# v of twelve attention pairs as two scaled 16-bit floats instead of three bfloat16 parts

## Chip, cores and metric

The kernel runs on one core of one Trainium2 chip. The metric is the device time of one execution in microseconds (us); three runs of the kernel before stand in the table below. A program is recorded ahead of time with a scheduling layer, which fixes the order of the instructions on every engine; on the chip each engine takes its own instructions strictly in that order and waits on semaphores for the others.

## The reference

Three blocks follow each other. Inputs are float32, the output is float32.

- Attention over 4 batches x 12 heads, 448 positions, head dimension 64, causal: `softmax(mask(q k^T / 8)) v`, with 1e-9 added to the sum of each row.
- A token and channel mixer on the result x (4 x 448 x 768): `u = x + (relu(x^T w_tok1) w_tok2)^T`, then `u + relu(u w_ch1) w_ch2`, with 1536 channels inside.
- A second mixer: `theta = x w_theta`, `y = w_tok_r (x cos theta) + w_tok_i (x sin theta)`, `u = x + y`, output `u + relu(u w_ch)`.

The change concerns the last product of the attention, attention weights times v, in half of its heads.

## The kernel before

Two heads of a batch make a pair, so there are 24 pairs, numbered 0 to 23 in order of batch. A pair has seven tiles of queries (`TILES`): one that holds the first 64 queries of both heads, and for each head three of 128 queries. The main loop goes through 24 x 7 = 168 steps. In each step the scores of one tile are computed (PE, L331 and L333), masked and reduced on DVE (L338), and put through the exponential on ACT (L340). Four steps later (`LAG`) the product with v of that tile is made (`pv`). After the seventh tile of a pair `finish` divides by the row sums, and after every second pair the token mixer (`tokmix`, L411 to L430) uses the result.

Between the steps stand the *units* of the channel mixer, each of 18 matmuls of 448 columns (L227 to L229), which fill PE. The same loop converts the weights (`round_first`, `round_bits`, `round_split`): they come in 64 bit, are rounded to float32 on ACT and DVE, scaled by a power of two found on the chip (`power`) and split into two float16 parts.

PE works in float32 only at a lower rate. So the pairs 0 to 11 multiply v as float32 (L375), and the pairs 12 to 23 work in pieces of 16 bit. There the weights of a tile are scaled by 2^15 and written as two float16 parts, "hi" by ACT (L157) and the rest by DVE (L360), into the tile `ph`; a transposing DMA on the SP queue brings them to `pt` (L363). v is cut into three bfloat16 parts (L296 to L301): the upper half of each float32 word is the first part and is read in place, DVE subtracts it into `v_mid` and the upper half of that is the second part, and DVE subtracts again for the third, in the lower half of `v_mid`. Per block of keys the product is then made of five matmuls of 64 columns (L386): hi with all three parts, the rest with the first two.

`v_raw` has two buffers and `v_mid` one; the parts of a pair are cut in `prep`, which is recorded in the first step of the pair before. `pv` and `scores` are recorded with high priority. `power` sums squares with matmuls of one column against ones, takes half the exponent on DVE (L140), inverts it (L127) and makes the factors on POOL (`product`, L130).

Of the kernel before, what the change touches and what calls it, by code (L numbers as in the profile page):

```python
# [18 lines left out]
P = 128  # L19
# [35 lines left out]
def fused(ctx, tc, q, k, v, w_tok1, w_tok2, w_ch1, w_ch2, w_theta, w_tok, w_ch, out):  # L55
# [73 lines left out]
    def product(dst, a, b, c):  # L129
        nc.gpsimd.tensor_scalar(out=dst, in0=a, scalar1=b, scalar2=c, op0=ALU.mult, op1=ALU.mult)  # L130

    def power(p, s, sq):

        ps = mm_bank()
        n = sq.shape[-1]
        nc.tensor.matmul(ps[:, 0:1], lhsT=ones, rhs=tiny, start=True, stop=False)
        for j in range(n):
            nc.tensor.matmul(ps[:, 0:1], lhsT=ones, rhs=sq[:, j:j + 1], start=False, stop=j == n - 1)
        g = main.tile([P, 2], F32, tag="g", name="g", bufs=4)
        nc.vector.tensor_scalar(out=g[:, 0:1].bitcast(U32), in0=ps[:, 0:1].bitcast(U32), scalar1=1, scalar2=EXPONENT,  # L140
                                op0=ALU.logical_shift_right, op1=ALU.bitwise_and)
        two_over(g[:, 1:2], g[:, 0:1])
        product(s, g[:, 1:2], 2.0 ** -51, 1.0)
        product(p, g[:, 0:1], 2.0 ** 64, 1.0)

    def largest(p, ps):
        nc.vector.tensor_reduce(out=p, in_=ps, axis=mybir.AxisListType.X, op=ALU.max)
# [119 lines left out]
    def prep(b, pr):  # L267
        qr = ap2.tile([P, 2 * S], F32, tag="qk_raw", name="q_raw", bufs=2)
        if b * NPR + pr in NATIVE:
            kr = ap2.tile([P, 2 * S], F32, tag="kh", name="k_pad")  # L270
            for t, src in ((kr, k), (qr, q)):
                (nc.vector if b * NPR + pr == 0 else nc.gpsimd).memset(t[64:128], 0.0)
                if b * NPR + pr == 0 and t is qr:
                    for c in (slice(0, 2 * P), slice(2 * P, 2 * S)):
                        nc.scalar.dma_start(out=t[0:64, c], in_=src[b, pr, 0:64, c])
                else:
                    loads[b * NPR + pr] = nc.sync.dma_start(out=t[0:64], in_=src[b, pr, 0:64])
        else:
            loads[b * NPR + pr] = nc.sync.dma_start(out=qr, in_=q[b, pr])
            kr = ap2.tile([P, 2 * S], F32, tag="qk_raw", name="k_raw", bufs=2)  # L280
            nc.sync.dma_start(out=kr, in_=k[b, pr])
        vr = ap2.tile([P, 9 * D], F32, tag="v_raw", name="v_raw")
        nc.sync.dma_start(out=vr, in_=v[b, pr])
        if b * NPR + pr in NATIVE:
            qs, kh, kl = qr, kr, None
        else:
            qs = ap2.tile([P, 2 * S], F32R, tag="qs", name="qs")
            copy_to(pick("qhi"), qs, qr)
            rest_to(pick("qlo"), qs[64:128], qr[64:128], qs[64:128])
            kh = ap2.tile([P, 2 * S], F32R, tag="kh", name="kh")  # L290
            copy_to(pick("khi"), kh, kr)
            kl = ap2.tile([P, 2 * S], F32R, tag="kl", name="kl")
            rest_to(pick("klo"), kl, kr, kh)
        if b * NPR + pr in NATPV:
            return qs, kh, kl, (vr,)
        v1 = vr.bitcast(BF16).rearrange("p (n w) -> p n w", w=2)[:, :, 1]  # L296
        vm = ap2.tile([P, 9 * D], F32, tag="v_mid", name="v_mid", bufs=1)
        rest_to(pick("v"), vm, vr, v1)
        v2, v3 = (vm.bitcast(BF16).rearrange("p (n w) -> p n w", w=2)[:, :, z] for z in (1, 0))
        rest_to(pick("v"), v3, vm, v2)  # L300
        return qs, kh, kl, (v1, v2, v3)  # L301

    TILES = ((0, 0), (1, 0), (1, 1), (2, 0), (2, 1), (3, 0), (3, 1))

    class Pair:
        def __init__(self, b, pr, parts):
            self.b, self.pr = b, pr
            self.qs, self.kh, self.kl, self.v = parts
            self.mx = ap2.tile([P, 7], F32, tag="mx", name="mx")
            self.sm = ap2.tile([P, 8], F32, tag="sm", name="sm")  # L310
            self.pts, self.ps, self.sent = {}, None, None
            self.native_pv = b * NPR + pr in NATPV
# [53 lines left out]
    def pv(pp, i, h):  # L366
# [9 lines left out]
                                 start=(u == 0), stop=(u == len(blks) - 1))  # L376
            return
        if i == 0:
            jobs = [(0, c, 8) for c in range(3)] + [(1, c, 8) for c in range(2)]
        else:  # L380
            jobs = [(0, c, 6 + h) for c in range(3)]
            for u in range(i):
                jobs += [(1 + u, c, 2 * u + h) for c in range(3)]
                jobs += [(1 + i + u, c, 2 * u + h) for c in range(2)]
        for n, (blk, c, vt) in enumerate(jobs):
            pp.pv = nc.tensor.matmul(pp.ps[:, reg:reg + D], lhsT=pt[:, blk], rhs=pp.v[c][:, vt * D:(vt + 1) * D],  # L386
                             start=(n == 0), stop=(n == len(jobs) - 1))

    def finish(pp, xb, xg):
        ps, sm = pp.ps, pp.sm  # L390
        nc.vector.tensor_scalar(out=sm[:, 0:7], in0=sm[:, 0:7], scalar1=1e-9, scalar2=1.0 if pp.native_pv else PSC, op0=ALU.add, op1=ALU.mult)
        nc.vector.reciprocal(out=sm[:, 0:7], in_=sm[:, 0:7])
        nc.vector.tensor_tensor(out=xb[:, 1:4, :].rearrange("p i (h d) -> p (i h) d", h=2),
                                in0=ps[:, D:7 * D].rearrange("p (j d) -> p j d", d=D),
# [205 lines left out]
    for n, (b, pr, t) in enumerate(steps):  # L600
# [24 lines left out]
        if t == 0 and (b, pr) != (B - 1, NPR - 1):  # L625
            nx = (b + (pr + 1) // NPR, (pr + 1) % NPR)
            with tc.high_priority(AHEAD), ExitStack() as es:
                if nx == (0, 1):
                    es.enter_context(tc.issue_after(loads[0].ins))
                parts[nx] = prep(*nx)  # L630
        if n >= LAG:
            with tc.high_priority(AHEAD):
                late_step(n - LAG)
            with tc.issue_after(pairs[steps[n - LAG][0:2]].pv.ins):
                for j, (at_step, _) in enumerate(ROUNDINGS):
                    if at_step == n - ROUND_SPLIT:
# [316 lines left out]
```

## Time and profile before

| | |
|---|---|
| time, median of 3 runs | 905.37 us (903.42 to 909.47) |
| the profiled execution | 907.62 us, of which the span from the first to the last instruction is 905.8 us |
| mean granted clock of TensorE | 0.981 of full speed |
| busy | PE 868.4 us (96%), DVE 632.0, ACT 538.1, POOL 166.0 |
| products of the twelve pairs in pieces (L386) | 996 matmuls, from 222.9 to 529.8 us |

PE is the matmul engine (TensorE), PEld its loading of the stationary operand, DVE the vector engine, ACT the scalar engine, POOL is GpSimd, SP only issues DMAs. A row `out<-in xcount` names what is written and read; L386 is line 386 of the kernel. Matmuls overlap, so the time that one costs is the distance between the starts of neighbours, not its duration. "PEclk" in a row of stretches is the granted clock as a share of 2.4 GHz; there are two levels, 2.4 and 1.2 GHz, and a value between is a mean over both.

### The profile page before, as it was taken

The page shows a single profiled execution, that of the slowest core. Times are in us where ns is not written, and L with a number is a line of the kernel's source. Part 1 is how long each engine was busy: PE and PEld are TensorE (multiplying, and loading weights), DVE is VectorE, ACT ScalarE, POOL GpSimd, SP SyncE. Part 2 cuts the span into 40 slices and gives each one's busy share as a digit, 9 for nine tenths or more (in the row PEclk, how much of TensorE's full clock was granted, in tenths as well). Part 3 has the DMA queues.
Part 4 walks back from the last instruction along what each step waited for, and adds up shares of the span by engine and source line. Part 5 has one row for each costly group of instructions (what it writes and reads, how often), then busy time and mean ns, then how long its engine had stood idle before and what let it go on. Part 6 is the DMA issues. An engine that isn't in the chain of part 4 may idle for free.

```text
span 905.8 us, 16756 instructions
## 1 busy us (share of the span) xinstructions
PE 868.4 (96%) x5979; PEld 563.7 (62%) x5979; DVE 632.0 (70%) x1499; ACT 538.1 (59%) x1247; POOL 166.0 (18%) x313
## 2 busy tenths in 40 slices
PE   7999699998988999899999998999999999999998
PEld 6888567776755667565666564556555555555554
DVE  7899867979997776738686328767875557566442
ACT  6788766767765654546573328546755457566441
POOL 3142322314141110101211102052211001101000
PEclk9999989999899999999999999999999999999999
DMA  7867745767799986747448568740440231231011
GB/s 225 243 194 237 281 166 194 259 210 202 211 279 319 261 204 140 202 110 193 142 103 224 162 195 298 258 131 10 145 143 29 86 114 39 92 114 45 21 57 72
DMA packets 105795, 149.67 MB, mean 165 GB/s; under 512 B 61104, under 2 KB 72304, under 8 KB 105712
## 3 DMA queue, kind: packets, MB, share of 16 engines
q1 hardware_dynamic: 105168, 147.59, 54.4%
q0 software_dynamic: 384, 0.79, 0.4%
q8 instruction: 47, 0.77, 0.4%
q14 instruction: 36, 0.29, 0.1%
q10 hardware_dynamic: 160, 0.23, 0.1%
HBM read 112.39 MB, written 22.81 MB: 149 GB/s over the span
## 4 chain that ended last, share of the span: by engine, by line
PE 74%; DVE 10%; DMA 8%; ACT 3%; issue 3%; POOL 1%; SPq 1%; DVEq 0%; ACTq 0%; POOLq 0%
PE ps_mm L228 17%; PE ps_mm L227 17%; PE ps_mm L229 17%; DMA pt<-ph 4%; PE ps_sc L229 3%; PE ps_sc L227 3%; PE ps_sc L228 3%; PE ps_pv L375 3%; PE ps_sc L331 2%; PE ps_pv L386 2%; PE ps_mm L347 2%; DVE sb L338 1%; PE ps_sc L333 1%; DVE wf L181 1%; DMA ws<-w_c 1%
## 5 line engine op out<-in xcount | busy, mean ns | idle before, releaser
L227 PE MATMUL ps_mm<-h,ws 128*128 128x448 f16 x432 | 152.8, 356 | 2.8 <-DMA ws<-w_c 2.8
L228 PE MATMUL ps_mm<-h,ws 128*128 128x448 f16 x432 | 153.4, 356 | 0.0
L229 PE MATMUL ps_mm<-h,ws 128*128 128x448 f16 x432 | 153.2, 356 | 0.0
L227 PEld LDWEIGHTS <-ws 128*128 128x128 f16 x720 | 71.1, 99 | 70.0 <-issue 5.7
L227 PE MATMUL ps_mm<-ut,ws 128*128 128x448 f16 x288 | 103.2, 359 | 8.8 <-ACT ut L157 8.2
L229 PEld LDWEIGHTS <-ws 128*128 128x128 f16 x720 | 71.1, 99 | 65.1 <-issue 5.2
L228 PEld LDWEIGHTS <-ws 128*128 128x128 f16 x720 | 71.1, 99 | 62.1 <-issue 4.9
L340 ACT ACTIVATE sb<-sb,mx 128x320 f32<-128x320 f32 (+3 forms) x168 | 89.3, 533 | 26.8 <-DVE mx L338 22.6
L228 PE MATMUL ps_mm<-ut,ws 128*128 128x448 f16 x288 | 103.0, 358 | 0.3 <-DVE ut L193 0.3
L229 PE MATMUL ps_mm<-ut,ws 128*128 128x448 f16 x288 | 102.8, 357 | 0.0
L338 DVE CUSTOM_DVE_ANT_0 sb<-ps_sc,mask 128x320 f32<-128x320 f32 (+3 forms) x168 | 73.8, 454 | 13.2 <-PE ps_mm L347 8.8
L124 ACT ACTIVATE junk<-acc 128x448 bf16<-128x448 f32 x72 | 41.2, 572 | 61.6 <-DVE acc L845 40.7
L375 PE MATMUL ps_pv<-v_raw,ptf 128*128 128x128 f32 (+1 forms) x456 | 63.2, 276 | 1.9 <-DVE x L398 1.7
L375 PEld LDWEIGHTS ps_pv<-v_raw,ptf 128*128 128x128 f32 x456 | 58.8, 191 | 6.9 <-ACT sb L340 1.9
L459 ACT ACTIVATE t<-ps_mm,c_scale 128x448 f32<-128x448 f32 x48 | 30.0, 628 | 54.5 <-PE ps_mm L229 45.9
L160 POOL TENSOR_SCALAR h<-t 128x448 f16<-128x448 f32 x48 | 31.3, 653 | 150.6 <-ACT t L459 150.3
L461 DVE TENSOR_TENSOR h<-t,h 128x448 f16<-128x448 f32 x48 | 31.3, 654 | 37.6 <-POOL h L160 37.5
L360 DVE SCALAR_TENSOR_TENSOR ph<-sb,ph 128x64 f16<-128x64 f32 (+3 forms) x156 | 43.0, 321 | 16.4 <-ACT ph L157 16.1
L157 ACT ACTIVATE ph<-sb 128x192 f16<-128x192 f32 (+3 forms) x84 | 36.5, 442 | 29.3 <-DMA pt<-ph 28.5
L130 POOL TENSOR_SCALAR f<-p_w,c_h 128x1 f32<-128x1 f32 x48 | 24.6, 516 | 145.2 <-DVE acc L473 129.0
L473 DVE SCALAR_TENSOR_TENSOR acc<-ps_mm,f,acc 128x448 f32<-128x448 f32 x48 | 32.4, 678 | 25.1 <-PE ps_mm L229 24.9
L227 PE MATMUL ps_sc<-th,ut 128*128 128x384 f16 x144 | 46.9, 326 | 0.0
(210 smaller groups left out, 2118.4 us busy)
## 6 DMA issues: line engine op xcount, KB each, us to landing
ws<-w_c SPq DMA_DIRECT2D x120, 384.0 KB, 4.0
raw<-in_w_ch_dram SPq DMA_DIRECT2D x30, 768.0 KB, 4.5
w_c<-ws SPq DMA_DIRECT2D x30, 384.0 KB, 3.8
q_raw<-in_q_dram SPq DMA_DIRECT2D x16, 448.0 KB, 3.6
k_raw<-in_k_dram SPq DMA_DIRECT2D x16, 448.0 KB, 5.6
v_raw<-in_v_dram SPq DMA_DIRECT2D x24, 288.0 KB, 3.4
x2d<-acc SPq DMA_DIRECT2D x24, 224.0 KB, 3.2
acc<-x2d SPq DMA_DIRECT2D x24, 224.0 KB, 2.9
```

Source lines behind the costliest of these rows:

```text
L124: nc.scalar.activation(j[:, 0:src.shape[-1]], src, AF.Square, accum_out=dst)
L157: nc.scalar.activation(dst, src, AF.Copy, scale=scale)
L160: e.tensor_scalar(out=dst, in0=src, scalar1=scale, scalar2=0.0, op0=ALU.mult, op1=ALU.add)
L227: nc.tensor.matmul(ps, lhsT=ka(a[:, 0]), rhs=kb(b[:, 0]), start=first, stop=False)
L228: nc.tensor.matmul(ps, lhsT=ka(a[:, 0]), rhs=kb(b[:, 1]), start=False, stop=False)
L229: return nc.tensor.matmul(ps, lhsT=ka(a[:, 1]), rhs=kb(b[:, 0]), start=False, stop=last)
L338: pp.first = nc.vector.tensor_tensor_reduce(out=dst, in0=src, in1=msk, op0=ALU.add, op1=ALU.min, scale=-0.125, scalar=3.0e38, accum_out=pp ...
L340: pp.last = nc.scalar.activation(sb[:, 0:kk], sb[:, 0:kk], AF.Exp, bias=pp.mx[:, j:j + 1], scale=-1.0, accum_out=pp.sm[:, j:j + 1])
L360: nc.vector.scalar_tensor_tensor(out=dst, in0=sb[:, c0:c1], scalar=PSC, in1=hi[:, c0:c1], op0=ALU.mult, op1=ALU.subtract)
L375: pp.pv = nc.tensor.matmul(pp.ps[:, reg:reg + n], lhsT=pt[:, u], rhs=pp.v[0][:, vt * D:vt * D + n], start=(u == 0), stop=(u == len(blks) - 1))
L461: gates[0] = nc.vector.tensor_tensor(out=t[:, 1], in0=f, in1=t[:, 0], op=ALU.subtract)
L473: nc.vector.scalar_tensor_tensor(out=acc[d], in0=ps[:, 0:S], scalar=f, in1=acc[d], op0=ALU.mult, op1=ALU.add)
```

## The change

For the pairs 12 to 23, v is scaled by a power of two and cut into two float16 parts instead of three bfloat16 parts. The sum of squares of the pair's v comes from ACT (`value_squares`, recorded in step 2 of the pair before), and `value_split`, recorded in step 4, finds the power of two (two matmuls of one column on PE, two rows on DVE, two products on POOL), lets POOL write the scaled upper part into `v_hi` (two buffers), and lets DVE write the rest in one operation into the lower halves of the words of `v_raw`. `pv` then makes three products per block instead of five: hi with both parts of v, the rest with the first. The factor 2^15, by which `finish` multiplied the row sums, becomes a column `unit` made on POOL. The two subtractions of `prep` go. The pairs 0 to 11 stay as they are.

```diff
@@ -129,7 +129,7 @@
     def product(dst, a, b, c):
         nc.gpsimd.tensor_scalar(out=dst, in0=a, scalar1=b, scalar2=c, op0=ALU.mult, op1=ALU.mult)
 
-    def power(p, s, sq):
+    def power(p, s, sq, unit=None):
 
         ps = mm_bank()
         n = sq.shape[-1]
@@ -141,7 +141,10 @@
                                 op0=ALU.logical_shift_right, op1=ALU.bitwise_and)
         two_over(g[:, 1:2], g[:, 0:1])
         product(s, g[:, 1:2], 2.0 ** -51, 1.0)
-        product(p, g[:, 0:1], 2.0 ** 64, 1.0)
+        if p is not None:
+            product(p, g[:, 0:1], 2.0 ** 64, 1.0)
+        if unit is not None:
+            product(unit, g[:, 1:2], 2.0 ** -51, PSC)
 
     def largest(p, ps):
         nc.vector.tensor_reduce(out=p, in_=ps, axis=mybir.AxisListType.X, op=ALU.max)
@@ -293,19 +296,34 @@
             rest_to(pick("klo"), kl, kr, kh)
         if b * NPR + pr in NATPV:
             return qs, kh, kl, (vr,)
-        v1 = vr.bitcast(BF16).rearrange("p (n w) -> p n w", w=2)[:, :, 1]
-        vm = ap2.tile([P, 9 * D], F32, tag="v_mid", name="v_mid", bufs=1)
-        rest_to(pick("v"), vm, vr, v1)
-        v2, v3 = (vm.bitcast(BF16).rearrange("p (n w) -> p n w", w=2)[:, :, z] for z in (1, 0))
-        rest_to(pick("v"), v3, vm, v2)
-        return qs, kh, kl, (v1, v2, v3)
+        return qs, kh, kl, (vr,)
+
+    values = {}
+
+    def value_squares(n):
+        sq = main.tile([P, 1], BF16, tag="sqv", name="sqv", bufs=2)
+        squares(sq, parts[n][3][0])
+        values[n] = sq
+
+    def value_split(n):
+
+        vr = parts[n][3][0]
+        sc = main.tile([P, 2], F32, tag="sv", name="sv", bufs=3)
+        scale, unit = sc[:, 0:1], sc[:, 1:2]
+        power(None, scale, values.pop(n), unit)
+        hi = ap2.tile([P, 9 * D], F16, tag="v_hi", name="v_hi", bufs=2)
+        copy_to("P", hi, vr, scale)
+        lo = vr.bitcast(F16).rearrange("p (n w) -> p n w", w=2)[:, :, 0]
+        nc.vector.scalar_tensor_tensor(out=lo, in0=vr, scalar=scale, in1=hi, op0=ALU.mult, op1=ALU.subtract)
+        parts[n] = (*parts[n][:3], (hi, lo), unit)
 
     TILES = ((0, 0), (1, 0), (1, 1), (2, 0), (2, 1), (3, 0), (3, 1))
 
     class Pair:
         def __init__(self, b, pr, parts):
             self.b, self.pr = b, pr
-            self.qs, self.kh, self.kl, self.v = parts
+            self.qs, self.kh, self.kl, self.v = parts[:4]
+            self.unit = parts[4] if len(parts) > 4 else 1.0
             self.mx = ap2.tile([P, 7], F32, tag="mx", name="mx")
             self.sm = ap2.tile([P, 8], F32, tag="sm", name="sm")
             self.pts, self.ps, self.sent = {}, None, None
@@ -376,19 +394,18 @@
                                  start=(u == 0), stop=(u == len(blks) - 1))
             return
         if i == 0:
-            jobs = [(0, c, 8) for c in range(3)] + [(1, c, 8) for c in range(2)]
+            jobs = [(0, 0, 8), (0, 1, 8), (1, 0, 8)]
         else:
-            jobs = [(0, c, 6 + h) for c in range(3)]
+            jobs = [(0, 0, 6 + h), (0, 1, 6 + h)]
             for u in range(i):
-                jobs += [(1 + u, c, 2 * u + h) for c in range(3)]
-                jobs += [(1 + i + u, c, 2 * u + h) for c in range(2)]
+                jobs += [(1 + u, 0, 2 * u + h), (1 + u, 1, 2 * u + h), (1 + i + u, 0, 2 * u + h)]
         for n, (blk, c, vt) in enumerate(jobs):
             pp.pv = nc.tensor.matmul(pp.ps[:, reg:reg + D], lhsT=pt[:, blk], rhs=pp.v[c][:, vt * D:(vt + 1) * D],
                              start=(n == 0), stop=(n == len(jobs) - 1))
 
     def finish(pp, xb, xg):
         ps, sm = pp.ps, pp.sm
-        nc.vector.tensor_scalar(out=sm[:, 0:7], in0=sm[:, 0:7], scalar1=1e-9, scalar2=1.0 if pp.native_pv else PSC, op0=ALU.add, op1=ALU.mult)
+        nc.vector.tensor_scalar(out=sm[:, 0:7], in0=sm[:, 0:7], scalar1=1e-9, scalar2=pp.unit, op0=ALU.add, op1=ALU.mult)
         nc.vector.reciprocal(out=sm[:, 0:7], in_=sm[:, 0:7])
         nc.vector.tensor_tensor(out=xb[:, 1:4, :].rearrange("p i (h d) -> p (i h) d", h=2),
                                 in0=ps[:, D:7 * D].rearrange("p (j d) -> p j d", d=D),
@@ -628,9 +645,18 @@
                 if nx == (0, 1):
                     es.enter_context(tc.issue_after(loads[0].ins))
                 parts[nx] = prep(*nx)
+        nx = b * NPR + pr + 1
+        nxt = (nx // NPR, nx % NPR)
+        split_next = nx < B * NPR and nx not in NATPV
+        if t == 2 and split_next:
+            with tc.issue_after(pairs[b, pr].last.ins):
+                value_squares(nxt)
         if n >= LAG:
             with tc.high_priority(AHEAD):
                 late_step(n - LAG)
+            if t == 4 and split_next:
+                with tc.issue_after(pairs[steps[n - LAG][0:2]].pv.ins), tc.high_priority(AHEAD // 2):
+                    value_split(nxt)
             with tc.issue_after(pairs[steps[n - LAG][0:2]].pv.ins):
                 for j, (at_step, _) in enumerate(ROUNDINGS):
                     if at_step == n - ROUND_SPLIT:
```

Two places in the recorded order. The first is on PE, at the first products of pair 15 with v; `wt` are weights of the token mixer, `ws` those of a unit, and `ps_sc<-kh,qs` are scores of the next pair. Before:

```order
L228 MATMUL ps_mm<-wt_181,h_3626 128x448
L229 MATMUL ps_mm<-wt_181,h_3626 128x448
L386 LDWEIGHTS pt
L386 MATMUL ps_pv<-v_raw,pt 128x64
L386 LDWEIGHTS pt
L386 MATMUL ps_pv<-v_mid,pt 128x64
L331 MATMUL ps_sc<-kh,qs 128x256
L331 MATMUL ps_sc<-kh,qs 128x320
```

and now:

```order
L230 LDWEIGHTS ws
L230 MATMUL ps_mm<-ut,ws 128x448
L403 LDWEIGHTS pt
L403 MATMUL ps_pv<-v_hi,pt 128x64
L231 LDWEIGHTS ws
L231 MATMUL ps_mm<-ut,ws 128x448
L232 LDWEIGHTS ws
L232 MATMUL ps_mm<-ut,ws 128x448
```

Before, the first two products (of hi with the first and the second part of v) stood behind the last products of the token mixer; now one product with `v_hi` stands between units, the second product (with the rest, in `v_raw`) follows after six matmuls of units, and the matmul of `sqv` for this pair stands 28 matmuls of units ahead of the first.

The second place is on DVE, at the split of v of pair 19. Before, two subtractions between the rests of the weights (`ph`) of the pair that runs:

```order
L164 TENSOR_TENSOR v_mid<-v_raw 128x576
L360 SCALAR_TENSOR_TENSOR ph<-sb_182,ph 128x64
L360 SCALAR_TENSOR_TENSOR ph<-sb_182,ph 128x384
L338 ISA sb_184,mx<-ps_sc,mask 128x448
L338 ISA mx 128x1
L338 ISA sb_186,mx<-ps_sc,mask_177 128x128
L338 ISA mx 128x1
L164 TENSOR_TENSOR v_mid<-v_mid 128x576
L164 TENSOR_TENSOR kl<-k_raw,kh 128x896
```

and now:

```order
L140 TENSOR_SCALAR g<-ps_mm 128x1
L127 TENSOR_SCALAR g<-g 128x1
L167 TENSOR_TENSOR kl<-k_raw,kh 128x896
L408 TENSOR_SCALAR sm<-sm,sv 128x7
L167 TENSOR_TENSOR qs<-q_raw,qs 64x896
L317 SCALAR_TENSOR_TENSOR v_raw<-v_raw,sv,v_hi 128x576
L409 RECIPROCAL sm<-sm 128x7
```

The split is one row, behind the two rows of `power` (`g`) and the rests of the split of k and q for the pair after; it reads `v_hi`, which POOL writes from `sv`.

## Rows read from the trace of the kernel before

**Rows 1.** The page: busy time, share of the span and count of each engine.

```profile
PE 868.4 (96%) x5979; PEld 563.7 (62%) x5979; DVE 632.0 (70%) x1499; ACT 538.1 (59%) x1247; POOL 166.0 (18%) x313
```

**Rows 2.** Stretches: us, busy of PE, PEld, DVE, ACT, POOL (count), clock, DMA share, GB/s.

```profile
219.00:281.00 62.00, 51.72 (x463) 36.30 (x462) 59.43 (x154) 43.56 (x106) 18.63 (x25) 0.89 0.90 244
281.00:300.00 19.00, 19.00 (x133) 13.40 (x132) 12.63 (x33) 9.77 (x27) 0.93 (x2) 0.91 1.10 352
300.00:530.00 230.00, 225.61 (x1879) 144.16 (x1878) 143.59 (x393) 117.96 (x290) 29.32 (x65) 0.99 0.66 169
350.00:375.00 25.00, 22.73 (x236) 15.08 (x233) 17.08 (x56) 14.17 (x36) 1.17 (x3) 0.93 0.82 166
```

**Rows 3.** The same for line L386 alone: busy of PE and PEld.

```profile
219.00:281.00 62.00, 10.15 (x231) 9.06 (x231) 0.89 0.90 244
281.00:530.00 249.00, 27.79 (x765) 25.98 (x765) 0.98 0.69 183
```

**Rows 4.** Longest waits of PE between 219 and 530 us: us in total, times, longest.

```profile
PE ps_pv L386 <- DMA pt<-ph: 7.8, 5, 3.4
PE ps_mm L227 <- DMA ws<-w_c: 2.8, 1, 2.8
PE ps_pv L386 <- issue: 2.0, 1, 2.0
PE ps_mm L412 <- DVE xg L164: 0.9, 1, 0.9
PE ps_sc L331 <- DVE mx L338: 0.4, 2, 0.2
```

**Rows 5.** The same waits between 219 and 281 us, those for `pt`.

```profile
PE ps_pv L386 <- DMA pt<-ph: 3.8, 2, 3.4
```

**Rows 6.** The chain of waits in that stretch: start, us, what.

```profile
403.23 1.40 PE ps_pv L386 x47
...
476.47 1.06 PE ps_pv L386 x36
```

**Rows 7.** Groups by form: busy us, mean ns of one, idle before and its releaser.

```profile
L193 DVE SCALAR_TENSOR_TENSOR ws<-wf,s,ws 128x768 f16<-128x768 f32 x30 | 30.8, 1025 | 9.5 <-POOL ws L160 6.3 <-ACT ws L157 3.1
L193 DVE SCALAR_TENSOR_TENSOR ut<-acc,s_u,ut 128x448 f16<-128x448 f32 x24 | 15.3, 676 | 0.9 <-ACT ut L157 0.9
L164 DVE TENSOR_TENSOR v_mid<-v_mid 128x576 bf16<-128x576 f32 x12 | 9.9, 824 | 0.0
L164 DVE TENSOR_TENSOR v_mid<-v_raw 128x576 f32<-128x576 f32 x12 | 9.0, 752 | 0.7 <-PE ps_pv L386 0.5
L160 POOL TENSOR_SCALAR h<-t 128x448 f16<-128x448 f32 x48 | 31.3, 653 | 150.6 <-ACT t L459 150.3
L160 POOL TENSOR_SCALAR ws<-wf,s 128x768 f16<-128x768 f32 x24 | 26.7, 1114 | 2.3
L124 ACT ACTIVATE junk<-wf 128x768 bf16<-128x768 f32 x30 | 25.1, 837 | 3.9 <-DVE wf L182 2.8 <-DVE g L127 0.9
```

**Rows 8.** PE in order of time around a `power`: start, us, instruction.

```profile
510.90 0.17 PE L136 MATMUL ps_mm<-tiny,ones 128*128 128x1 bf16 x1
510.93 0.16 PE L138 MATMUL ps_mm<-sqb,ones 128*128 128x1 bf16 x1
510.95 0.35 PE L227 MATMUL ps_mm<-ut,ws 128*128 128x448 f16 x1
511.14 0.35 PE L228 MATMUL ps_mm<-ut,ws 128*128 128x448 f16 x1
```

**Rows 9.** Instructions of one product of POOL between 219 and 530 us: ns min/median/max.

```profile
L130 POOL TENSOR_SCALAR s<-g x10: 185/190/1566, 219.9 to 511.6; 128x1 f32<-128x1 f32 x10
```

**Rows 10.** In order of time: a split behind a `power` on full queues.

```profile
245.18 0.15 DVE L140 TENSOR_SCALAR g<-ps_mm 128x1 uint32<-128x1 uint32 x1
...
249.88 1.30 DVE L193 SCALAR_TENSOR_TENSOR ws<-wf,s,ws 128x768 f16<-128x768 f32 x1 [0.40 <-POOL ws L160]
```

**Rows 11.** Waits between 219 and 530 us: us in total, times, longest.

```profile
ACT ph L157 <- DMA pt<-ph: 28.5, 28, 3.0
```

## The prediction

> **What bounds the kernel now.** I read the page first: PE is busy for 96% of the span [rows 1], so at first sight every matmul that goes is time won. But the share is a mean, and the products that change all lie between 219 and 530 us. The table of stretches there [rows 2] shows two stages. From 219 to 281 us PE is busy for 51.7 of 62 us and DVE for 59.4: PE stands for 10.3 us, DVE for 2.6, and the DMA engines have a share of 0.90. That stage is not PE's. From 281 us on it is: PE is busy for all of 19 us, and for 225.6 of 230 us after that. The same table for the line of the products alone [rows 3] says how they are divided: 231 of the 996 in the first stage, 765 in the second. The list of PE's waits [rows 4] says what ends them: most of all the DMA that brings the transposed weights `pt` (7.8 us in five waits), then two single waits of 2.8 and 2.0 us. No wait for `v_mid` is among them.
>
> **The change, part by part.**
>
> *Products.* A pair has one tile with 5 products, and two each with 8, 13 and 18: 83. With three a block these become 3, 5, 8 and 11: 51. Twelve pairs lose 384 of 996, 38.6%. One costs the distance to the next: 47 in 1.40 us and 36 in 1.06 us [rows 6], 29.8 and 29.4 ns; I take 29.6. In the second stage 295 of the 765 go: 295 x 29.6 ns = 8.7 us. In the first stage 89 go, at 10.15 us / 231 = 44 ns (some ran at the lower clock) 3.9 us; but there PE has 10.3 us of idle time already, DVE sets the pace, and I count nothing.
>
> *What waits give back.* Shorter PE work arrives earlier at a wait whose end PE does not set. Of the five waits for `pt`, two with 3.8 us lie in the first stage [rows 5], so three with 4.0 us in the second. Each such wait swallows about what one pair saves, 32 x 29.6 ns = 0.95 us: 2.8 us. At least it is nothing, at most all ten pairs' savings; the latter is a rival below.
>
> *The search for the power of two, on PE.* Two matmuls of one column per pair. In the row of such a `power` three starts follow at 510.90, 510.93 and 510.95 us [rows 8]: 0.05 us a pair, 0.5 us for the ten pairs of the second stage.
>
> *DVE.* Two subtractions go, 752 and 824 ns [rows 7]. One operation with a scale comes: between 676 ns at 448 columns and 1025 at 768 [rows 7], 576 columns make 816. The two rows of `power` add 0.15 us each [rows 10]. Net 1.58 - 1.12 = 0.46 us less a pair. In the second stage DVE is busy for 156 of 249 us, so this is hidden. In the first stage, with 231/83 = 2.8 pairs, it would be 1.3 us on the path. Against it stands a new wait: the operation reads what POOL writes, and waits at its place in DVE's queue, with scores, weights and `acc` behind it. The nearest row, the same operation behind POOL's copy of weights, idles 6.3 us in 24 cases, 0.26 us each [rows 7]; the most is POOL's whole copy. 2.8 pairs x 0.26 to 0.84 us is 0.7 to 2.4 us. So the first stage comes out between 0.6 us won and 1.1 lost, and I take nothing.
>
> *POOL.* The copy to `v_hi` lies between 653 ns at 448 columns and 1114 at 768 [rows 7]: 0.84 us; two products of one column add 0.19 us each where nothing disturbs them and up to 1.57 us where something does [rows 9]. POOL is busy for 18.6 of 62 and 30 of 249 us [rows 2], so its time is hidden. What is behind the copy in its queue are copies of units and factors; it matters only as a link in the chain of the second rival.
>
> That spread on POOL has a reason in the notes. The Trainium skill, "SBUF — State Buffer", section "Who interferes with whom", says that a vector instruction with two SBUF inputs and a GpSimd instruction that reads SBUF cannot run together: who comes first holds the shared port for its whole instruction. The spread from 185 to 1566 ns for one and the same product agrees with it. By that rule the three copies of the first stage also hold up DVE, about 2.4 us in all by the copy's estimate above, and the sum below would be 3.0 instead of 5.4 us. That lies inside the forecast's own range, and its chance is part of it: the rows show no vector operation with two inputs held up for so long, the subtractions of v average 752 and 824 ns [rows 7].
>
> *ACT.* A sum of squares over 576 columns takes less than the 837 ns of 768 columns [rows 7]. ACT is busy for 44 of 62 us and 128 of 249 [rows 2]; hidden. *SP.* No DMA is added or removed; loads and transposes go past each other a little differently. *finish* multiplies by a column instead of a constant, in the same instruction: nothing.
>
> *Sum.* -8.7 + 0.5 + 2.8 + 0 = -5.4 us. Against the profiled execution: span 905.8 to 900.4, its time of 907.6 to 902.2. That run lies 2.2 us above the median, so by the median 905.4 becomes 900.0.
>
> **The rivals.**
>
> *All of it arrives (about 892 us).* PE's waits for `pt` do not grow, since ACT and DVE get their scores earlier too and start the transposes earlier, and in the first stage a freer PE shortens the chain. Then 8.7 + 3.9 - 0.6 = 12.0 us. In addition the clock: the stretch from 350 to 375 us, with a wait of PE in it, shows a granted clock of 0.93 [rows 2], so 3.5 of 25 us at the lower level, which costs PE 1.7 us of work. One or two such dips fewer would make it 13.7 to 15.4. For it: PE busy for 98% in the second stage. Against it: DMA shares of 0.9 and 1.1 up to 300 us [rows 2], which no matmul changes. 890 to 895 us.
>
> *PE stands before the new parts of v (about 917 us).* In the order, 28 matmuls of units lie between the matmul of the squares and the first product of a pair, and 6 more before the product that needs the rest. At 0.19 us each [rows 8] that is 5.3 and 6.4 us. On free queues the chain takes two rows of DVE, two of POOL, the copy and the scaled subtraction: 0.30 + 0.38 + 0.84 + 0.82 = 2.3 us. On full queues the like of it for weights took from 245.18 to 251.18 us, 6.0 us [rows 10], with one POOL product less. And DVE's queue holds rests of weights that wait for ACT, which waits for the transposing DMA up to 3.0 us [rows 11]: 9.0 us, 2.6 late. PE takes its rows in order, so all units behind stand as well, and a dip of the clock as above follows: 2.6 + 1.7 = 4.3 us a pair. It decides from a chain of 6.4 us on; one or two late pairs cancel the gain, and four of the ten make 4 x 4.3 - 5.4 = 11.8 us more: 917. Against it: before, a pair's first two products and its third were placed around two DVE operations in the same manner, and PE never waited for them [rows 4]; and after 300 us the queues of POOL and DVE are mostly free [rows 2].
>
> *Nothing arrives (905 to 906 us).* After 281 us the transposes, not PE, pace the pairs; every saving becomes a longer wait for `pt`, and the search costs 0.5 us. For it: five waits of up to 3.4 us for just that DMA, and ACT stops 28 times for the same transposes [rows 4, 11]. Against it: between those waits units fill PE without a gap.
>
> **How the numbers follow.** Partly hidden, as in the sum (897 to 903): 0.45. All of it: 0.22. Nothing: 0.18. PE stands: 0.15. The likeliest gives 900.0. The range runs from 891.5, which leaves out the better part of the first rival, to 909.5, which leaves out the slower one from about two late pairs on; outside lie some 0.06 and 0.13. One per cent, 9 us, is about what a measurement of this kernel can tell from no change. Faster by more (below 896.3): the first rival and a little of the forecast, 0.25. Slower by more (above 914.4): two thirds of the second, 0.10. Within: 0.65.
>
> **What would show it.** The products should number 612 at some 30 ns, ending some 5 us earlier than 529.8; waits for `pt` after 281 us should have grown from 4 to about 7 us; PE should have no wait, or one under a microsecond, for `v_hi` or `v_raw`. A stage up to 281 us that is shorter by more than 2 us, or waits for `pt` that have not grown, speaks for the first rival. Waits of PE for DVE or POOL at the start of pairs speak for the second. I am wrong if new PE work, such as slower products or one-column matmuls that wait for ACT, takes what the 384 gave.

## The result, and the profile after

The changed kernel takes **894.32 us** (median of 4 runs, 892.61 to 895.83) where the kernel before, run beside it, takes 905.39 (903.42 to 909.47): a ratio of 0.9887, with a 95% interval from 0.9861 to 0.9913. That is 11.1 us or 1.1% less, and the interval leaves out 1. The profiled executions stand 13.6 us apart, spans of 892.2 and 905.8 us.

The page's first line, to be held against [rows 1]:

```profile
PE 856.9 (96%) x5619; PEld 551.0 (62%) x5619; DVE 631.9 (71%) x1511; ACT 543.7 (61%) x1271; POOL 180.9 (20%) x349
```

PE does 360 matmuls less (384 products fewer, 24 one-column matmuls more) and is busy for 11.5 us less. DVE's total is the same to 0.1 us; POOL has 14.9 us more.

The same stretches as in [rows 2], with the end moved from 530 to 515 us, where the products now end (columns: us, busy of PE, PEld, DVE, ACT, POOL with counts, granted clock, DMA share, GB/s):

```profile
219.00:281.00 62.00, 52.28 (x371) 33.63 (x370) 58.57 (x149) 42.29 (x103) 18.62 (x30) 0.86 0.90 250
281.00:300.00 19.00, 19.00 (x143) 13.87 (x142) 13.24 (x39) 12.96 (x37) 1.86 (x6) 1.00 1.05 292
300.00:515.00 215.00, 210.74 (x1595) 132.24 (x1593) 145.29 (x400) 121.01 (x302) 41.53 (x89) 1.00 0.68 182
350.00:375.00 25.00, 25.00 (x204) 14.88 (x203) 16.89 (x47) 11.62 (x31) 3.83 (x9) 1.00 0.73 189
```

and for the line of the products alone, against [rows 3]:

```profile
219.00:281.00 62.00, 5.60 (x124) 4.69 (x125) 0.86 0.90 250
281.00:516.00 235.00, 19.40 (x489) 17.51 (x488) 1.00 0.71 191
```

The products number 613 here (one at the border is in both rows); the profile has 612. Their busy time fell by 4.6 us in the first stage and by 8.4 in the second. PE's idle time in the first stage is 9.7 us, where it was 10.3: it did not grow by what the products gave up, so other matmuls moved forward into that time.

PE's longest waits between 219 and 530 us (us in total, times, longest), against [rows 4]:

```profile
PE ps_mm L230 <- DMA ws<-w_c: 4.4, 1, 4.4
PE ps_sc L349 <- DVE mx L356: 3.1, 4, 1.4
PE ps_mm L230 <- DVE h L432: 2.0, 1, 2.0
PE ps_pv L403 <- DVE x L415: 2.0, 1, 2.0
PE ps_pv L403 <- DMA pt<-ph: 1.8, 3, 1.4
PE ps_pv L403 <- DVE v_raw L317: 0.3, 1, 0.3
```

The wait for the transposed weights `pt`, 7.8 us in five waits in the kernel before, is down to 1.8 in three. It was the largest wait and is now the fifth. The scores' wait for `mx` grew from 0.4 to 3.1 us. Only one wait, of 0.3 us, is for the new parts of v.

ACT's wait for the same transposes between 219 and 530 us, against [rows 11]:

```profile
ACT ph L160 <- DMA pt<-ph: 44.4, 36, 7.6
```

ACT waits for them longer, 44.4 us where it was 28.5; it is PE that no longer stands there.

Groups by form (busy us, mean ns, idle before and its releaser), against [rows 7]:

```profile
L317 DVE SCALAR_TENSOR_TENSOR v_raw<-v_raw,sv,v_hi 128x576 f16<-128x576 f32 x12 | 11.4, 950 | 0.3 <-POOL v_hi L163 0.2
L163 POOL TENSOR_SCALAR v_hi<-v_raw,sv 128x576 f16<-128x576 f32 x12 | 11.3, 940 | 0.0
L124 ACT ACTIVATE junk<-v_raw 128x576 bf16<-128x576 f32 x12 | 8.1, 676 | 1.7 <-DMA v_raw<-in_v_dram 1.6
```

The scaled subtraction takes 950 ns (estimated 816), the copy on POOL 940 (840), the sum of squares 676. They lie on engines that have room.

A pair in order of time, pair 15, where the first product comes soonest after the search (start, us, engine, instruction):

```profile
295.28 0.16 PE L138 MATMUL ps_mm<-sqv,ones 128*128 128x1 bf16 x1
...
295.79 0.15 DVE L140 TENSOR_SCALAR g<-ps_mm 128x1 uint32<-128x1 uint32 x1
...
296.21 0.34 POOL L130 TENSOR_SCALAR sv<-g 128x1 f32<-128x1 f32 x2 [1.77 <-DVE g L127]
...
296.53 0.74 POOL L163 TENSOR_SCALAR v_hi<-v_raw,sv 128x576 f16<-128x576 f32 x1
...
300.60 0.19 PE L403 MATMUL ps_pv<-v_hi,pt 128*128 128x64 f16 x1
...
301.31 0.85 DVE L317 SCALAR_TENSOR_TENSOR v_raw<-v_raw,sv,v_hi 128x576 f16<-128x576 f32 x1
...
302.21 0.19 PE L403 MATMUL ps_pv<-v_raw,pt 128*128 128x64 f16 x1 [0.28 <-DVE v_raw L317]
```

`v_hi` is ready at 297.3 us, 3.3 us ahead of its first product. The rest is ready just as its product wants it: PE stands for 0.28 us. That is the only place where it does.

### The profile page after: what moved, and what is told of

Its sections match the earlier page's. It is cut to its first block, busy times and chain, and to the rows that moved or that the text cites. A ratio compares the mean times of both kernels' runs of the same rounds, so it can differ in the third digit from the quotient of the medians.

```text
span 892.2 us, 16092 instructions
## 1 busy us (share of the span) xinstructions
PE 856.9 (96%) x5619; PEld 551.0 (62%) x5619; DVE 631.9 (71%) x1511; ACT 543.7 (61%) x1271; POOL 180.9 (20%) x349
## 4 chain that ended last, share of the span: by engine, by line
PE 71%; DVE 13%; DMA 8%; ACT 4%; issue 3%; POOL 2%; SPq 0%; DVEq 0%; ACTq 0%; POOLq 0%
PE ps_mm L230 16%; PE ps_mm L231 16%; PE ps_mm L232 16%; PE ps_pv L393 3%; PE ps_sc L349 3%; DMA ws<-w_c 3%; PE ps_sc L231 2%; PE ps_sc L230 2%; PE ps_sc L232 2%; DMA pt<-ph 2%; PE ps_mm L365 2%; DVE wf L184 1%; DVE sb L356 1%; PE ps_pv L403 1%; DVE ut L196 1%
## 5 line engine op out<-in xcount | busy, mean ns | idle before, releaser
L230 PE MATMUL ps_mm<-ut,ws 128*128 128x448 f16 x288 | 104.5, 363 | 11.4 <-ACT ut L160 6.9
L358 ACT ACTIVATE sb<-sb,mx 128x192 f32<-128x192 f32 (+3 forms) x168 | 89.3, 533 | 35.5 <-DVE mx L356 31.5
L231 PE MATMUL ps_mm<-ut,ws 128*128 128x448 f16 x288 | 104.3, 362 | 1.2 <-DVE ut L196 1.2
L232 PE MATMUL ps_mm<-ut,ws 128*128 128x448 f16 x288 | 104.0, 361 | 0.0
L356 DVE CUSTOM_DVE_ANT_0 sb<-ps_sc,mask 128x192 f32<-128x192 f32 (+3 forms) x168 | 74.1, 454 | 13.5 <-PE ps_mm L365 10.1
L378 DVE SCALAR_TENSOR_TENSOR ph<-sb,ph 128x64 f16<-128x64 f32 (+3 forms) x156 | 45.5, 335 | 25.6 <-ACT ph L160 25.2
L349 PE MATMUL ps_sc<-kh,qs 128*128 128x256 f32 (+2 forms) x112 | 45.7, 413 | 3.3 <-DVE mx L356 3.1
L130 POOL TENSOR_SCALAR f<-p_w,c_h 128x1 f32<-128x1 f32 x48 | 21.5, 450 | 126.7 <-DVE acc L490 91.6
L476 ACT ACTIVATE t<-ps_mm,c_scale 128x448 f32<-128x448 f32 x48 | 29.7, 621 | 28.3 <-PE ps_mm L232 25.2
```

What stands on the lines that cost most here:

```text
L230: nc.tensor.matmul(ps, lhsT=ka(a[:, 0]), rhs=kb(b[:, 0]), start=first, stop=False)
L231: nc.tensor.matmul(ps, lhsT=ka(a[:, 0]), rhs=kb(b[:, 1]), start=False, stop=False)
L232: return nc.tensor.matmul(ps, lhsT=ka(a[:, 1]), rhs=kb(b[:, 0]), start=False, stop=last)
L349: nc.tensor.matmul(ps[:, 0:n], lhsT=lhs, rhs=cut(pp.kh), start=True, stop=pp.kl is None)
L356: pp.first = nc.vector.tensor_tensor_reduce(out=dst, in0=src, in1=msk, op0=ALU.add, op1=ALU.min, scale=-0.125, scalar=3.0e38, accum_out=pp ...
L358: pp.last = nc.scalar.activation(sb[:, 0:kk], sb[:, 0:kk], AF.Exp, bias=pp.mx[:, j:j + 1], scale=-1.0, accum_out=pp.sm[:, j:j + 1])
```

## The experiments

All times are medians; ratios are against the kernel before, run on the same chip in the same series (its medians there: 904.75 to 905.99 us). From the span on, a row is that of the one profiled run: "clock" is its mean granted clock; "products" is their number and the sum of the distances from a product's start to the next matmul's start, idle left out; PE's idle time is summed from its first to its last matmul; the waits are those from 219 to 545 us; "ahead" is how many matmuls of scores, counted from the pair's own first and with those of the next pair, stand in PE's order ahead of a pair's first product, a mean over the pairs in pieces.

| kernel | us | ratio, 95% interval | span | clock | products | PE idle | waits for `pt` | waits for `mx` | ahead |
|---|---|---|---|---|---|---|---|---|---|
| before | 905.39 |  | 905.8 | 0.981 | 996, 32.0 us | 28.6 | 7.8 | 0.4 | 20.2 |
| changed | 894.32 | 0.9887, 0.9861 to 0.9913 | 892.2 | 0.983 | 612, 18.9 | 26.2 | 1.8 | 3.1 | 22.9 |
| three_all | 904.70 | 1.0003, 0.9982 to 1.0024 | 899.1 | 0.985 | 612, 21.2 | 33.4 | 9.7 | 2.8 | 20.7 |
| three_first | 909.65 | 1.0045, 1.0022 to 1.0068 | 910.5 | 0.984 | 900, 28.8 | 35.2 | 11.6 | 1.9 | 20.8 |
| three_late | 899.81 | 0.9943, 0.9922 to 0.9964 | 898.1 | 0.987 | 708, 23.2 | 31.5 | 8.6 | 0.4 | 20.2 |
| after_five | 904.36 | 0.9991, 0.9977 to 1.0005 | 903.9 | 0.992 | 996, 31.7 | 29.7 | 2.2 | 8.4 | 24.0 |
| hi_one | 895.10 | 0.9890, 0.9857 to 0.9924 | 893.0 | 0.983 | 612, 18.6 | 27.2 | 1.8 | 2.7 | 22.9 |
| bf16_buf2 | 901.70 | 0.9960, 0.9937 to 0.9984 | 898.9 | 0.983 | 612, 21.3 | 31.2 | 8.5 | 5.3 | 20.2 |
| after_early | 894.75 | 0.9877, 0.9835 to 0.9919 | 891.8 | 0.983 | 612, 19.3 | 25.5 | 4.3 | 1.7 | 20.8 |
| after_const | 906.36 | 1.0009, 0.9990 to 1.0027 | 905.6 | 0.975 | 612, 20.9 | 33.5 | 11.1 | 3.3 | 20.3 |
| const_later | 901.62 | 0.9962, 0.9928 to 0.9996 | 903.2 | 0.981 | 612, 20.7 | 33.6 | 1.0 | 5.6 | 22.5 |
| bf16_later | 894.76 | 0.9884, 0.9852 to 0.9916 | 891.4 | 0.986 | 612, 19.9 | 28.6 | 1.2 | 5.3 | 22.7 |
| after_later | 899.26 | 0.9917, 0.9891 to 0.9942 | 898.1 | 0.987 | 612, 19.8 | 31.7 | 5.5 | 6.9 | 23.0 |
| before_later | 911.69 | 1.0068, 1.0045 to 1.0091 | 912.5 | 0.983 | 996, 32.5 | 34.2 | 4.1 | 5.4 | 22.5 |

The profiled run of three_all lies 3.9 us below its median, so its row shows it too well; those of before, three_first, const_later and before_later lie 2.2 to 3.3 us above theirs. What is left of a span beside products and idle time lies between 842.5 and 851.2 us and goes in good part with the granted clock: it is largest in after_const, which has the lowest clock of the table, and smallest in after_five, which has the highest.

**The count alone, in the kernel before.** Three kernels leave out the products with the third part of v, in all twelve pairs, in the pairs before 15, and in those from 15 on. The split itself and its two subtractions stay.

```diff
+        few = 1        # three_first: int(pp.b * NPR + pp.pr < 15); three_late: >= 15
-            jobs = [(0, c, 6 + h) for c in range(3)]
+            jobs = [(0, c, 6 + h) for c in range(3 - few)]
-                jobs += [(1 + u, c, 2 * u + h) for c in range(3)]
-                jobs += [(1 + i + u, c, 2 * u + h) for c in range(2)]
+                jobs += [(1 + u, c, 2 * u + h) for c in range(3 - few)]
+                jobs += [(1 + i + u, c, 2 * u + h) for c in range(2 - few)]
```

> The kernel before, with three of the five products per block in all twelve pairs (hi with the first two parts of v, the rest with the first; the third part of v is still cut, but not used, so the output is less exact). 384 products go, v is cut as before. If the whole count arrives at the end: 384 x 29.6 ns = 11.4 us less, about 894. If the first stage and the waits for the transposed weights swallow what my sum gave them: 5.9 less, about 899.5. If the new order and the second buffer of v made the gain, not the count: within 2 us of 905.4.

> The kernel before, with three of five products (as in the run with all twelve pairs) only in the pairs 12 to 14, which lie mostly before 281 us; 96 products go. My sum counted nothing there, since DVE and the DMA engines set the pace: 905.4. If they arrive all the same: 96 x 29.6 to 44 ns, 2.8 to 4.2 us less, about 902.

> The kernel before, with three of five products only in the pairs 15 to 23; 288 products go, 8.5 us. If waits for the transposed weights give back 2.8 us, as in my sum: 5.7 less, about 899.7. If all arrive: about 897. If shorter waits also bring fewer stretches of the lower clock: 894 to 896.

PE's waits in three_all, 219 to 545 us, and those for `pt` after 281 us alone:

```profile
PE ps_pv L387 <- DMA pt<-ph: 9.7, 15, 2.6
...
PE ps_sc L331 <- DVE mx L338: 2.8, 4, 1.3
```

```profile
PE ps_pv L387 <- DMA pt<-ph: 3.4, 8, 0.9
```

and in three_late, 219 to 545 us:

```profile
PE ps_pv L387 <- DMA pt<-ph: 8.6, 9, 4.0
```

The same 384 products that go in the changed kernel gain nothing here (1.0003). PE waits fifteen times for `pt` instead of five, and between the first and the 400th matmul of the units it stood 4.9 us more than in the kernel before. In the first pairs alone the cut costs 4.5 us, in the later ones it gains 5.4; the two together come near three_all. So waits can swallow the count, and in this recorded order they do. They do not do it where the prediction put them, though: after 281 us the waits for `pt` did not grow in three_all (3.4 us, 3.9 in the kernel before). That three_late came out as the sum had it (899.8, forecast 899.7) is luck: after 281 us its waits for `pt` are 3.8 us, and its idle time grew earlier, where its products are still the old ones (13.3 us between the first and the 400th matmul of the units, 10.6 in the kernel before).

**The split alone, with five products.** The changed kernel gets its two products per block back; they multiply a tile of zeros.

```diff
+    none = ac.tile([P, D], F16, tag="none", name="none")
+    nc.gpsimd.memset(none, 0.0)
-        parts[n] = (*parts[n][:3], (hi, lo), unit)
+        parts[n] = (*parts[n][:3], (hi, lo, none), unit)
-                jobs += [(1 + u, 0, 2 * u + h), (1 + u, 1, 2 * u + h), (1 + i + u, 0, 2 * u + h)]
+                jobs += [(1 + u, 0, 2 * u + h), (1 + u, 1, 2 * u + h), (1 + u, 2, 0), (1 + i + u, 0, 2 * u + h), (1 + i + u, 2, 0)]
```

> The changed kernel with two more products per block, hi and the rest each with a tile of zeros, so that the result stays the same and five products are made as before. If the count is the gain: back by 11.4 us, about 905.5. If waits swallow part: about 900. If the new way of cutting v makes the gain: about 895.

Its waits of PE:

```profile
PE ps_sc L351 <- DVE mx L358: 8.4, 13, 1.6
PE ps_pv L405 <- DMA pt<-ph: 2.2, 4, 1.2
```

The time is back at 904.36 us, 10.0 above the changed kernel. The new split and its search cost, with the order that they bring, nothing that can be measured (0.9991), and gain nothing either, though `pt` is waited for 2.2 us only: the scores' wait for DVE took its place. Here the count is worth 10 us, with two things not held fixed: the order is not quite that of the changed kernel (24.0 scores ahead, 22.9 there), and the granted clock was higher (0.992, 0.983 there), which cannot be what made it slower.

**The buffers, the step and the search.** hi_one gives `v_hi` one buffer instead of two. bf16_buf2 is three_all with a second part of its own in 16 bit and two buffers, and without the second subtraction. after_early records the search and the split one and two steps earlier. after_const has no search: the scale is 4096.

```diff
# hi_one
-        hi = ap2.tile([P, 9 * D], F16, tag="v_hi", name="v_hi", bufs=2)
+        hi = ap2.tile([P, 9 * D], F16, tag="v_hi", name="v_hi", bufs=1)
# bf16_buf2
-        vm = ap2.tile([P, 9 * D], F32, tag="v_mid", name="v_mid", bufs=1)
+        v2 = ap2.tile([P, 9 * D], BF16, tag="v_mid", name="v_mid", bufs=2)
# after_early
-        if t == 2 and split_next:
+        if t == 1 and split_next:
-            if t == 4 and split_next:
+            if t == 2 and split_next:
# after_const
-        power(None, scale, values.pop(n), unit)
+        scale, unit = 4096.0, 4096.0 * PSC
```

> The changed kernel with one buffer for the upper part of v in place of two. Theory A: the gain needs both, fewer products and the later place of a pair's first products, which now wait in the order for parts of v that are made late and so find the transposed weights there (PE's waits for them 1.8 us against 7.8 before, 9.7 with three products in the old arrangement). Then the buffer does not matter: 893 to 896, waits for the transposed weights under 3 us. Rival B: it is the second buffer, which lets the split of the next pair go on before the products of this one are done; then about 903.

> The kernel before with three products per block of two bfloat16 parts, the second cut by one subtraction into its own tile with two buffers, at the old early place; no search for a power of two (the third part is left out, so the output is less exact). Theory A: the parts are there early, the products go early in the order and PE waits for the transposed weights, 8 us or more: 900 to 905. Rival B (the second buffer): about 894, or 893, since no search is needed.

> The changed kernel with the squares recorded in step 1 instead of 2 of the pair before and the split in step 2 instead of 4. Theory A: earlier parts let the products go earlier in the order, and waits for the transposed weights come back, in all or in part: 896 to 903, these waits 4 us or more. Rival B: no change, about 894. Rival C (the chain of the search is late at the products, so earlier is better): 891 to 893.

> The changed kernel with the constant factors 2^12 and 2^27 in place of those found on the chip (no squares, no matmuls of one column, no products on POOL), the copy and the subtraction at the same place of the program. The search by itself costs 12 x 0.05 us on PE. If nothing else of it is on the path: 893.5 to 894.5. Theory A, since without the chain the parts are there some 2 us earlier: a little of the waits comes back, 894 to 897. If the chain holds PE up: 890 to 892.

hi_one has the same order on PE, matmul by matmul, and the same time within the intervals: the second buffer is not the cause. bf16_buf2 gains 4.3 of the 11 us. after_const, which does strictly less than the changed kernel, loses the whole gain:

```profile
PE ps_pv L399 <- DMA pt<-ph: 11.1, 8, 4.2
...
PE ps_sc L345 <- DVE mx L352: 3.3, 5, 1.8
```

Its waits for `pt` are the largest but for three_first's (11.6), and no expectation had such a time. A part of the loss is the clock. The two longest of these waits, of 2.5 and 4.2 us, lie in two stretches with a granted clock of 0.86:

```profile
300.00:325.00 25.00, 20.63 (x162) 12.28 (x160) 15.98 (x54) 12.92 (x36) 2.94 (x6) 0.86 0.93 199
355.00:380.00 25.00, 20.84 (x163) 12.94 (x162) 17.45 (x56) 13.09 (x35) 3.10 (x4) 0.86 0.79 165
```

In the changed kernel the clock is 1.00 in both. PE was busy for 10.9 us at the lower of the two levels there, and half of that, some 5.4 us by estimate, is what the lower level costs, beside the waits themselves. Without the search the scheduling layer puts a pair's first product behind 20.3 matmuls of scores, nearly as in the kernel before (20.2), instead of 22.9. That made the place of the products in PE's order the next suspect.

**The place of the products.** Four kernels lower the priority with which the products of the pairs in pieces are recorded, together with `finish` and the parts of the token mixer that are recorded in the same step, and change nothing else: after_const, bf16_buf2, the changed kernel and the kernel before.

```diff
-            with tc.high_priority(AHEAD):
+            with tc.high_priority(AHEAD - (350 if steps[n - LAG][0] * NPR + steps[n - LAG][1] not in NATPV else 0)):
                 late_step(n - LAG)
```

> The kernel with constant factors (no search; 906.4 us, 11.1 us of waits of PE for the transposed weights), with the priority of the products of pairs 12 to 23 lowered from 500 to 150, so that the order puts a pair's first product later: on the mean behind 22.5 matmuls of scores counted from the pair's own first, as against 20.3 with constant factors before and 22.9 in the changed kernel. Theory A (place and count together make the gain): waits for the transposed weights 5 us or less, 893 to 897. Rival D (the chain of the search itself spreads the work of DVE and POOL better, or the difference is another accident of the order): 901 to 906.

> The kernel before with three products per block of two bfloat16 parts in two buffers (901.7 us, 8.5 us of waits for the transposed weights), with the same lowered priority; first products behind 22.7 matmuls of scores, 20.2 without. Theory A: waits 5 us or less, 893 to 897. Rival D: 900 to 904.

> The changed kernel with the same lowered priority: first products behind 23.0 matmuls of scores, 22.9 without. Theory A: the place hardly moves, so the time hardly does: 892 to 896. Rival D says nothing here; if it is slower than 898, the order decides in some other way than by this place.

> The kernel before, with all five products, and only the priority of the products of pairs 12 to 23 lowered from 500 to 150, as in the run of two bfloat16 parts that came to 894.8 us. Theory A (count and place together): the place alone removes waits for the transposed weights but leaves the work, 902 to 907. Rival E (the place alone is the gain, the count nothing): 893 to 897.

PE's waits in bf16_buf2, and then in bf16_later:

```profile
PE ps_pv L386 <- DMA pt<-ph: 8.5, 12, 1.6
PE ps_sc L330 <- DVE mx L337: 5.3, 8, 1.8
```

```profile
PE ps_sc L330 <- DVE mx L337: 5.3, 7, 3.2
...
PE ps_sc L330 <- DVE g L127: 3.1, 1, 3.1
...
PE ps_pv L386 <- DMA pt<-ph: 1.2, 2, 0.9
```

The same products, later in the order: the waits for `pt` go from 8.5 to 1.2 us and the time from 901.70 to 894.76, the changed kernel's. That is the order at work, without scale or search. The waits for `pt` are not all of it: of the 7.5 us between the two profiled spans only 2.6 are idle time of PE and 1.4 products; the rest goes with a higher granted clock (0.986, 0.983 in bf16_buf2). And const_later, against after_const, gains less:

```profile
PE ps_sc L345 <- DVE mx L352: 5.6, 10, 1.5
PE ps_sc L345 <- DVE g L127: 3.1, 1, 3.1
...
PE ps_pv L399 <- DMA pt<-ph: 1.0, 1, 1.0
```

Its waits for `pt` went from 11.1 to 1.0 us, its time only from 906.36 to 901.62, and PE's idle time did not fall at all (33.5 and 33.6 us): the scores now wait for DVE. And before_later, the kernel before with its five products put later, became slower:

```profile
PE ps_sc L331 <- DVE mx L338: 5.4, 5, 2.3
PE ps_pv L386 <- DMA pt<-ph: 4.1, 2, 3.9
```

So the later place alone gives nothing; it costs 6 to 7 us there. after_later shows that later is not always better (899.26 us, 4.9 above the changed kernel, with 5.5 us for `pt`), and after_early, whose products stand at 20.8, is as fast as the changed kernel at 22.9.

## Why the prediction was right and wrong

The time lies inside the range, but the likeliest case did not occur: 900.0 was forecast as "partly hidden", and 894.3 is where the first rival stood, which had a chance of 0.22; its own sum without dips of the clock, 12.0 us, gives 893.4. "Faster by more (below 896.3)" had 0.25. Both signs that the prediction named for this rival came: the first stage is 3.0 us shorter, and the waits for `pt` have not grown. That the range holds the time is thus owed to its being wide enough for a rival, not to the sum. Nor is the rival's reason shown, that transposes start earlier because ACT and DVE get their scores earlier.

*Products: right.* The sum has 8.7 us less in the second stage; their busy time there fell by 8.4 us. Their distance stayed what [rows 6] gave. The chain of waits in the changed kernel has, for instance,

```profile
354.12 0.82 PE ps_pv L403 x28
...
359.85 0.64 PE ps_pv L403 x22
```

29.3 and 29.1 ns a product.

*First stage: wrong.* "[...] but there PE has 10.3 us of idle time already, DVE sets the pace, and I count nothing." The 400th matmul of the units started at 288.8 us instead of 291.8, with no less of PE's other work done: 3.0 us of the gain were made by then, near the 3.9 that the products there give up. Idle time of PE in a stretch is no sign that its work there is free; it was made up of a few long waits, such as the two for `pt` [rows 5], and between them matmuls stood close enough for the work behind to move up. The kernels on the count show that it can as well be worse: cut in the first pairs alone, the same products cost 4.5 us.

*"What waits give back": this step failed.* It put "2.8 us" on three waits for `pt`, each swallowing what a pair saves. After 281 us those waits fell from 3.9 us to 0.4, and PE's idle time between 219 us and the end of the products went from 14.7 to 14.0 us: nothing was given back. The mechanism as such is real, in other orders: after 281 us, where the kernel before has 3.9 us of waits for `pt`, bf16_buf2 has 8.1 and after_const 10.4. What I missed is that the change also rewrites the order. I had shown that the first product of a pair moves from behind the mixer's products to between units, and used it for the second rival alone; whether it thereby moves behind the arrival of `pt` as well, I did not ask.

*The search, POOL, ACT, SP: right within 0.3 us on PE.* The one-column matmuls cost 0.8 us against 0.5. The new rows on DVE and POOL were underestimated by 12 to 16%, without effect. The rule of the Trainium skill ("SBUF — State Buffer", "Who interferes with whom"), by which the copies on POOL would hold up DVE in the first stage, is not seen in the time: DVE's busy time there is 58.6 us, where it was 59.4, and that stage became shorter. Single rows are held up in that manner; the last section shows them.

*finish: "nothing"* was mis-sized, but the time is hidden: see the last section.

*The balance* of the profiled spans: products -13.1, one-column matmuls +0.8, idle time -2.4, everything else +1.1, together -13.6 us. The first rival's extra for dips of the granted clock came in the second stage and was lost again elsewhere. Between the 400th and the 1200th matmul of the units the kernel before took 228.2 us and the changed one 217.3: 10.9 us less, of which products make 8.0, idle time 0.1 and all else 2.9. There the kernel before has two stretches at the lower level, each behind a wait for `pt` (2.3 and 1.3 us): the one that the prediction named [rows 2] and one more; the changed kernel has none. At the prediction's 1.7 us each that is 3.4 us. But the changed kernel was at the lower level for longer in the first stage (0.86, it was 0.89), and once more behind its products, where the kernel before has 1.00. First the kernel before, then the changed one:

```profile
420.00:445.00 25.00, 23.33 (x165) 13.37 (x164) 17.06 (x50) 14.89 (x39) 4.30 (x9) 0.93 0.42 110
```

```profile
525.00:545.00 20.00, 17.73 (x97) 8.89 (x96) 15.18 (x34) 15.12 (x33) 3.46 (x9) 0.91 0.88 278
```

Over the whole span the units' distances sum to 408.2 us, where they were 408.1. Nor does the clock make the gain of the medians: the four runs of the changed kernel had a mean granted clock of 0.980 to 0.983, the 23 of the kernel before beside the first experiments 0.980 to 0.991.

*The other rivals.* "Nothing arrives" is the time of three_all, not of the changed kernel; even there the waits for `pt` after 281 us did not grow. "PE stands before the new parts of v" was wrong: one wait of 0.28 us. The chain from the squares to the rest took 6.9 us in the tightest pair, 0.28 of them a wait of PE; the point from which it decides, 6.4 us, was set nearly right, and one pair passed it.

**What stays open.** Shown is that the gain needs the smaller count (after_five; no kernel with 996 products has a median under 904 us), that the count alone is worth anything from nothing (three_all, after_const) to the whole gain, and that the recorded order decides between them: a priority alone moves the same instructions by 6.9 us (bf16_later) or by 4.9 the other way (after_later). Not shown is which property of the order decides: the number of scores ahead does not (after_early), nor do the waits for `pt` alone (const_later). "Theory A" of the expectations, by which a later place of the products removes the waits for `pt` and so makes the gain, came true in three of its eight forecasts (hi_one, bf16_buf2, bf16_later) and missed the time in the other five. The lowered priority also moves `finish` and the token mixer, and no run separates them from the products. The wait that takes the place of that for `pt`, most often that of the scores for DVE, depends on the whole recorded order. No version beats the changed kernel: hi_one, after_early and bf16_later are equal to it within their intervals, and bf16_later keeps less of v.

## What to carry to other kernels

Here work taken from the busiest engine paid only where the recorded order kept that engine fed; so besides the busy time, compare where the order puts the remaining work against the transfers that it waits for. Where a scheduling layer makes the order, an edit with no cost in instructions can move the time by more than half of what the edit under study does (901.7 to 894.8 us by a priority alone): try the count in more than one order before crediting or dismissing it. And a wait of the matmul engine can cost more than its length, where a stretch at the lower clock lies around or behind it; so read the granted clock beside the waits.

## What the runs showed of the hardware

One operation became slower. In `finish`, a row over 128x7 is multiplied by a constant, or by a column that POOL writes; first in after_const, where the factor is a constant again, then in the changed kernel (ns: least, median, most):

```profile
L404 DVE TENSOR_SCALAR sm<-sm x12: 156/162/727, 230.5 to 483.6; 128x7 f32<-128x7 f32 x12
```

```profile
L408 DVE TENSOR_SCALAR sm<-sm,sv x12: 217/707/716, 230.1 to 491.3; 128x7 f32<-128x7 f32 x12
```

With the column it takes some 0.71 us in seven of twelve cases and 0.22 in the others, against 0.16. The seven are those that start while POOL's copy to `v_hi` runs, and each ends 0.02 to 0.03 us after that copy; in the other five no such copy is running. One of either kind:

```profile
296.53 0.74 POOL L163 TENSOR_SCALAR v_hi<-v_raw,sv 128x576 f16<-128x576 f32 x1
296.59 0.71 DVE L408 TENSOR_SCALAR sm<-sm,sv 128x7 f32<-128x7 f32 x1 [0.47 <-POOL sv L130]
```

```profile
444.27 1.54 POOL L163 TENSOR_SCALAR v_hi<-v_raw,sv 128x576 f16<-128x576 f32 x1
445.88 0.22 DVE L408 TENSOR_SCALAR sm<-sm,sv 128x7 f32<-128x7 f32 x1
```

So the column itself costs some 0.06 us, and the rest, going by these ends, is DVE held up by POOL; no run was made to test it. The constant does not spare it: in the kernel before, three of the same twelve rows took 0.35 to 0.42 us, and each ended 0.03 us after a copy of POOL. In the changed kernel it adds about 4 us of DVE in all; none of PE's waits there ends with one of these rows.

The new rows of the split spread by a factor of two:

```profile
L163 POOL TENSOR_SCALAR v_hi<-v_raw,sv x12: 740/745/1579, 212.2 to 491.2; 128x576 f16<-128x576 f32 x12
L317 DVE SCALAR_TENSOR_TENSOR v_raw<-v_raw,sv,v_hi x12: 810/872/1535, 213.0 to 492.2; 128x576 f16<-128x576 f32 x12
```

Their medians, 745 and 872 ns, lie near the estimates; it is the few long cases, up to 1579 and 1535 ns, that make the means of 940 and 950. The four long copies on POOL (1106 ns and more) ran beside operations of DVE with two inputs, and the two long subtractions on DVE (1236 and 1535 ns) beside copies of POOL; the other eight copies took 740 to 747 ns.
